# The opening of a fused attention and feed-forward kernel in another order: loads, weight preparation and transposes

## The chip, the core and the metric

The kernel runs on one core of one Trainium2 chip. A core has five engines that work side by side, each through its own list of instructions: PE (TensorE, matrix products; its weight loads are listed as PEld), DVE (VectorE), ACT (ScalarE), POOL (GpSimd) and SP (SyncE, which here only issues transfers). Engines wait for each other and for transfers through semaphores. Transfers between the large memory (HBM) and the on-chip memory run on 16 DMA engines. The metric is the time of one execution on the device in microseconds (us); a kernel's time is the median of several runs.

## The reference

Two blocks follow each other. The first is attention without a softmax: for each of 8 batches and 8 heads, a 64 x 64 matrix kv is the product of k and v over the sequence, the output is q times kv, and each row of 64 is divided by its root mean square and scaled by g_norm. The second is a feed-forward block on the 4608 x 512 result.

```python
kv = np.einsum('bhsd,bhse->bhde', k, v)              # 8 x 8 x 576 x 64
out = np.einsum('bhsd,bhde->bhse', q, kv)
rms = np.sqrt(np.mean(out * out, axis=-1, keepdims=True) + 1e-06)
attn = out / rms * g_norm
x = attn.transpose(0, 2, 1, 3).reshape(B * S, H * D) # 4608 x 512
h = x @ w_in                                         # 512 x 2048
r = np.maximum(h, 0.0)
y = (r * r) @ w_out                                  # 2048 x 512
```

All arrays are float32 at the reference's boundary, and moe_w_in and moe_w_out reach the kernel as 64-bit words (I64 in the code): the random weights are divided by a double, so they are double-precision numbers, and the kernel makes float32 numbers of them itself.

## The kernel before

**Tiles.** Tokens are taken in strips of 512 (four tiles of 128; N_STRIP = 9). A strip goes up through W_in (products into PSUM banks A, B and C, then relu and square into gt tiles) and down through W_out. The products are formed in Strassen-like sums of quarters; only the first strip goes up plainly (up_first, matmul at L588), so that it needs nothing of W_in but the converted pieces. Heads are taken in pairs: p = 0 to 3 of a batch.

**The opening.** The first strip needs batch 0's four pairs. For one pair these slices exist:

- convert_on_act(p): ACT prepares piece p of W_in, an activation to w_c (L203) and one in place on raw (L206). A piece is 128 x 512 double-precision words, one transfer of 512 KB.
- transposed_query (T in the changed code): PE transposes q by a product with the identity into t_ps (L331), ACT copies it to qT (L333).
- key_value (K): PE forms kv_ps (L349), ACT copies its two diagonal blocks into kv_all (L351, L352).
- first_queries (Q): PE forms x_ps (L419), ACT squares it into sq (L384), DVE sums to ms (L386, L387). Here also the first two of four DVE steps of a piece's conversion are issued (L215, L217).
- first_normalized (N): a third step of the conversion (L221), then ACT's square root to rms (L392), DVE's reciprocal and a Newton step (L393 to L398), the scaled x_n (L430), and the last conversion step (L224), which writes w_in.
- first_features (F): PE transposes x_n into xt_ps (L440), ACT scales it into xT (L441).

The loop over p puts them into one list: convert_on_act(p), T(p), K(p), N(p-1), Q(p), F(p-1), and N(3), F(3) at the end. attend(n) issues the list up to place n. Every engine takes its own instructions in this order: the schedule is written by hand (tc.manual_schedule()), nothing is sorted later. Before the list's last two slices the kernel issues convert_on_act for pieces 4 and 5.

**Loads.** All go through SP's queue. load_next loads k, v and the two halves of q of the next pair; load_piece loads the next piece into one of 8 raw buffers. Before the opening: the rest rows of k and v, then pair p and piece p by turns, then load_more(0) up to 8 pieces. Eight semaphores serve these loads in turn, so that a load waits for the landing of the one eight places earlier. A piece's buffer is used again when its conversion is done.

**Beside the first strip.** During the 16 up_first steps, convert(5 + (3i + 2)//4) issues the conversion of further pieces two by two, first ACT's part for a pair ahead, then DVE's four steps; pieces 24 to 31 (W_out's second half) are combined by DVE (L241) and sent back to HBM (w_out). Also batch 1's T and K are issued in the last of these steps. The first product of the next stage (query, products_x with the matmul at L373) needs all of batch 1's kv_all copies.

**Buffers.** apsum has four PSUM buffers for t_ps, kv_ps, x_ps and xt_ps; wtmp has four for w_c; fpsum holds banks A (twice), B and C.

Of the kernel before, what the change touches and what calls it, by code (L numbers as in the profile page):

```python
# [19 lines left out]
def kernel(  # L20
# [36 lines left out]
    B, H, S, D = q.shape  # L57
# [3 lines left out]
    NP = H // 2  # L61
# [35 lines left out]
    def load(b, p, q_eng):  # L97
        hs = slice(2 * p, 2 * p + 2)
        if b == 0 and p >= 2:

            h_place = g_pool.tile([P, 4, C * P], FP32, name="first_qkv", tag="gt")
        for i, (n, src, eng) in enumerate((("k", k, nc.sync), ("v", v, nc.sync), ("q", q, q_eng))):
            whole = src[b, hs, 0 : C * P].rearrange("h (sp c) d -> sp h c d", c=C)
            if n == "q" and b >= Q_ON_PE:

                t = qkv_pool.tile([P, 4 * C, SQ], FP32, name=n, tag=n)
                for a in range(4):
                    h, f = divmod(a * SQ, D)
                    eng.dma_start(
                        out=t[ts(a, SQ)],  # L110
                        in_=src[b, 2 * p + h, 0 : C * P, f : f + SQ].rearrange("(i k) f -> i k f", k=4 * C),
                    )
            elif n != "q":
                if b == 0 and p >= 2:
                    t = h_place[:, i].rearrange("p (h c d) -> p h c d", h=2, c=C)
                else:
                    t = qkv_pool.tile([P, 2, C, D], FP32, name=n, tag=n)
                eng.dma_start(out=t, in_=whole)
            else:

                if b == 0 and p >= 2:
                    t = h_place[:, i].rearrange("p (c h d) -> p c h d", h=2, c=C)
                else:
                    t = qkv_pool.tile([P, C, 2, D], FP32, name=n, tag=n)
                for h in range(2):
                    eng.dma_start(out=t[:, :, h, :], in_=whole[:, h])
            main[n, b, p] = t
# [9 lines left out]
    def load_rest(b, eng):  # L137
        h = b % 2
        half = slice(REST * h, REST * (h + 1))
        for t, src in ((k_rest[half], k), (v_rest[half, h], v)):  # L140
            eng.dma_start(out=t, in_=src[b, :, C * P : S].rearrange("h s d -> s h d"))
# [20 lines left out]
    def load_next(q_eng=nc.sync):  # L162
        u = next(to_load, None)
        if u is not None:
            load(*u, q_eng)


    KH, FH, DH = NP // 2, d_ff // 2, d_model // 2
# [4 lines left out]
    w_in = wpool.tile([P, KH, NG, 7, WN // 2], FP32, name="w_in")  # L173
# [14 lines left out]
    def load_piece():  # L188
        if len(raw) < len(sources):
            t = raw_pool.tile([P, 2, WN // 2], I64, name="raw", tag="raw")  # L190
            nc.sync.dma_start(out=t, in_=sources[len(raw)])
            raw.append(t)
# [16 lines left out]
    def conversion(i, dest):  # L209

        c, r, high = words.pop(i)
        ci = c.bitcast(I32)


        yield nc.vector.tensor_scalar(out=c, in0=c, scalar1=LEAST, scalar2=MOST, op0=ALU.max, op1=ALU.min)  # L215

        yield nc.vector.tensor_scalar(  # L217
            out=ci, in0=ci, scalar1=3, scalar2=0x3FFFFFFF, op0=ALU.logical_shift_left, op1=ALU.bitwise_and
        )

        yield nc.vector.scalar_tensor_tensor(  # L221
            out=ci, in0=high, scalar=-(2**30), in1=ci, op0=ALU.bitwise_and, op1=ALU.bitwise_or
        )
        yield nc.vector.tensor_tensor(out=dest.bitcast(I32), in0=ci, in1=r, op=ALU.add)  # L224
# [71 lines left out]
    nc.scalar.sqrt(one, one)  # L296

    load_rest(0, nc.sync)
    for p in range(NP):
        load_next()  # L300
        load_piece()
    load_more(0)
# [7 lines left out]
    flat = lambda t: t.rearrange("p h d -> p (h d)")  # L310
# [70 lines left out]
    def mean_squares(ps):  # L381
        n = ps.shape[-1] // D
        sq = xn_pool.tile([P, d_model], FP32, name="sq", tag="sq", bufs=1)
        nc.scalar.activation(sq, ps, AF.Square)  # L384
        ms = small.tile([P, H], FP32, name="ms", tag="ms")
        nc.vector.reduce_sum(out=ms, in_=by_head(sq), axis=AX.X)  # L386
        nc.vector.tensor_scalar(out=ms, in0=ms, scalar1=1.0 / D, scalar2=EPS, op0=ALU.mult, op1=ALU.add)  # L387
        return ms

    def inverse_root(ms):  # L390
        r = small.tile([P, H], FP32, name="rms", tag="rms")
        nc.scalar.activation(r, ms, AF.Sqrt)  # L392
        nc.vector.reciprocal(r, r)  # L393

        t = small.tile([P, H], FP32, name="newton", tag="newton")
        nc.vector.scalar_tensor_tensor(out=t, in0=ms, scalar=-0.5, in1=r, op0=ALU.mult, op1=ALU.mult)
        nc.vector.tensor_tensor(out=t, in0=t, in1=r, op=ALU.mult)
        nc.vector.scalar_tensor_tensor(out=r, in0=t, scalar=1.5, in1=r, op0=ALU.add, op1=ALU.mult)  # L398
        return r
# [12 lines left out]

    first = {}

    def first_queries(p):

        ps = apsum.tile([P, NT, P], FP32, name="x_ps", tag="at")
        for n in range(NT):
            nc.tensor.matmul(ps[:, n, :], lhsT=qT[0, p][:, n, :], rhs=kvd[0, p], start=True, stop=True)  # L419
        steps = conversion(p, w_in[:, p % KH, 0, p // KH * 2 : p // KH * 2 + 2])  # L420
        next(steps)
        next(steps)
        first[p] = flat(ps), mean_squares(flat(ps)), steps

    def first_normalized(p):
        ps, ms, steps = first.pop(p)
        next(steps)
        x_n["first", p] = t = xn_pool.tile([P, NT, P], FP32, name="x_n", tag="x_n")
        r = inverse_root(ms)
        nc.vector.tensor_tensor(  # L430
            out=by_head(flat(t)), in0=by_head(ps), in1=r.unsqueeze(2).to_broadcast([P, H, D]), op=ALU.mult
        )
        for _ in steps:
            pass

    def first_features(p):
        t, x = x_n.pop(("first", p)), open_xt(0)
# [47 lines left out]
        minus(nc.vector, t4, x(1, 0), t2)  # L485

    slices, ready = [], {}
    for b in range(B):
        for p in range(NP):
            if b:  # L490
                slices += [(transposed_query, (b, p)), (key_value, (b, p))]
                continue

            slices += [(convert_on_act, (p,)), (transposed_query, (b, p)), (key_value, (b, p))]
            if p > 0:
                slices.append((first_normalized, (p - 1,)))
            slices.append((first_queries, (p,)))
            if p > 0:
                slices.append((first_features, (p - 1,)))
        first_n = b // 2 * PAIR + (C if b % 2 else 0)  # L500
        ns = list(range(first_n, first_n + C + b % 2))
        if b == 0:
            slices += [(first_normalized, (NP - 1,)), (first_features, (NP - 1,))]
            ready[0] = len(slices)
            continue
        for i in range(len(ns) + 1):
            if i < len(ns):
                slices.append((query, (ns[i],)))
            if 0 < i <= len(ns):
                slices.append((features if b < X_ON_PE else squares_x, (ns[i - 1],)))  # L510
            if i > 0 and ns[i - 1] % NT == NT - 1:
                ready[ns[i - 1] // NT] = len(slices)
    slice_at = [0]

    def attend(n):
        while slice_at[0] < min(n, len(slices)):
            fn, a = slices[slice_at[0]]
            fn(*a)
            slice_at[0] += 1
# [272 lines left out]
        if k == 6 and s + 1 < N_STRIP:  # L792
            sums_x(s + 1)

    attend(ready[0] - 2)
    for i in range(NP, NP + 2):
        convert_on_act(i)
    acted[0] = NP + 2
    for s in range(N_STRIP):
        attend(ready[s])  # L800
        if s == 0:
            steps = [(2, up_first, (g, fh, i)) for g in range(NG) for fh in range(2) for i in range(2)]
        else:
            steps = [(1, up, (s, g, p)) for g in range(NG) for p in ORDER]
# [85 lines left out]
```

## Time and profile before

| | |
|---|---|
| median of 9 runs | 964.82 us (963.02 to 967.02) |
| the profiled execution's own time | 963.02 us |
| its span in the profile | 961.2 us |
| PE, DVE, ACT busy | 927.8, 644.2, 229.0 us |
| first matmul | 10.11 us |
| first matmul of the first strip's up products (L588) | 37.74 us |
| first conversion step of piece 4 on DVE | 37.29 us |
| mean granted TensorE clock | 0.992 |

Times in the profile count from the start of the span. A line of the timeline gives an instruction's start, its length, its engine and source line, the tiles it writes and reads, and, in brackets, how long its engine had been idle before it and what ended that. In the waits, a line says which engine and line waited for which, in total, how often, and the longest. ACT and DVE show starts closer together than an instruction's length: neighbours overlap in their ends, so a chain of instructions is best counted from start to start.

| us | PE busy | DVE busy | ACT busy | granted clock | GB/s |
|---|---|---|---|---|---|
| 0 to 10 | 0.00 | 1.41 | 1.49 | 1.00 | 154 |
| 10 to 20 | 7.30 | 3.37 | 4.94 | 1.00 | 323 |
| 20 to 30 | 5.66 | 7.76 | 6.57 | 1.00 | 367 |
| 30 to 40 | 4.50 | 8.13 | 5.59 | 0.54 | 104 |
| 40 to 60 | 20.00 | 20.00 | 18.63 | 0.98 | 271 |
| 60 to 80 | 20.00 | 18.48 | 18.72 | 1.00 | 311 |
| 80 to 110 | 30.00 | 27.33 | 19.93 | 1.00 | 247 |

### The profile page before, as it was taken

Reading aid. Unit: us, or ns where it says so; the run is one execution under the profiler, and the core shown is the slowest. Engines: PE = TensorE matmul, PEld = TensorE weight load, DVE = VectorE, ACT = ScalarE, POOL = GpSimd, SP = SyncE. Lnnn points to the kernel's source line nnn. Section 1 sums busy time; section 2 is a strip of 40 time slices with the busy share of each in tenths; the row PEclk is TensorE's granted clock in tenths of the full one; section 3 lists DMA queues with packets and bytes.
Section 4 is the critical chain, followed back from the end, with each engine's and each line's share of the span. In section 5 each row is a group of like instructions: output and inputs, shape, how many; then the busy total and the mean of one; then the engine's idle time right before and its main releaser. Section 6 shows DMA issues by size and latency. Waiting matters only on the chain.

```text
span 961.2 us, 15319 instructions
## 1 busy us (share of the span) xinstructions
PE 927.8 (97%) x5976; PEld 816.4 (85%) x5976; DVE 644.2 (67%) x1161; ACT 229.0 (24%) x501; POOL 1.7 (0%) x7
## 2 busy tenths in 40 slices
PE   3699999999999999999999999999999999999996
PEld 3344888888888998899889998999889988998996
DVE  3899864585437875587648874787568655863583
ACT  3697441320023002210222012201220022002200
POOL 0000000000000000000000000000000000000000
PEclk9799999999999999999999999999999999999998
DMA  8699883536975485557563765467506721671064
GB/s 256 214 294 306 271 219 146 131 113 217 313 241 122 176 299 168 123 187 251 189 152 135 248 222 153 117 240 263 134 23 239 254 88 55 230 263 55 16 227 153
DMA packets 164520, 180.33 MB, mean 188 GB/s; under 512 B 85088, under 2 KB 138848, under 8 KB 155872
## 3 DMA queue, kind: packets, MB, share of 16 engines
q1 hardware_dynamic: 164288, 179.36, 59.2%
q8 instruction: 47, 0.77, 0.3%
q14 instruction: 25, 0.20, 0.1%
q10 hardware_dynamic: 160, 0.00, 0.0%
HBM read 148.11 MB, written 31.20 MB: 187 GB/s over the span
## 4 chain that ended last, share of the span: by engine, by line
PE 95%; ACT 2%; DVE 2%; DMA 1%; issue 0%; SPq 0%; DVEq 0%
PE ps_A L552 29%; PE ps_B L552 14%; PE ps_B L736 14%; PE ps_A L736 14%; PE ps_C L552 12%; PE ps_A L588 3%; PE x_ps L378 3%; PE kv_ps L349 2%; PE ps_B L588 1%; PE ps_C L588 1%; DMA raw<-in_moe_w_in_dram 1%; PE x_ps L373 0%; PE xt_ps L440 0%; ACT w_c L203 0%; ACT raw L206 0%
## 5 line engine op out<-in xcount | busy, mean ns | idle before, releaser
L552 PE MATMUL ps_A<-x_t,w_in 128*128 128x256 f32 x768 | 182.6, 381 | 1.3 <-DVE gt L611 1.3
L552 PEld LDWEIGHTS ps_A<-x_t,w_in 128*128 128x128 f32 x768 | 143.6, 190 | 21.1 <-DVE gt L611 2.1
L736 PE MATMUL ps_B<-w_blk,g_s 128*128 128x128 f32 x672 | 81.9, 275 | 0.0
L736 PE MATMUL ps_A<-w_blk,g_s 128*128 128x128 f32 x672 | 81.9, 275 | 0.0
L736 PEld LDWEIGHTS ps_B<-w_blk,g_s 128*128 128x128 f32 x672 | 78.4, 192 | 0.0
L736 PEld LDWEIGHTS ps_A<-w_blk,g_s 128*128 128x128 f32 x672 | 78.4, 192 | 0.0
L612 DVE SCALAR_TENSOR_TENSOR gt<-gt 128x512 f32<-128x512 f32 x96 | 66.4, 692 | 3.3
L562 ACT COPY snap<-ps_A 128x512 f32<-128x512 f32 x68 | 39.8, 585 | 113.8 <-PE ps_A L552 99.3
L611 DVE TENSOR_TENSOR gt<-ps_C,snap 128x512 f32<-128x512 f32 x32 | 22.0, 688 | 64.3 <-PE ps_C L552 64.3
L736 PE MATMUL ps_B<-w_blk,gt 128*128 128x128 f32 x504 | 63.1, 275 | 0.0
L736 PE MATMUL ps_A<-w_blk,gt 128*128 128x128 f32 x504 | 63.1, 275 | 0.0
L611 DVE TENSOR_TENSOR gt<-ps_A,snap 128x512 f32<-128x512 f32 x32 | 22.0, 687 | 60.4 <-PE ps_A L552 60.3
L552 PE MATMUL ps_A<-xT,w_in 128*128 128x256 f32 x256 | 61.2, 382 | 0.0
L552 PE MATMUL ps_C<-xT,w_in 128*128 128x256 f32 x256 | 61.0, 381 | 0.0
L552 PE MATMUL ps_B<-x_t,w_in 128*128 128x256 f32 x256 | 60.9, 381 | 0.0
L241 DVE TENSOR_TENSOR gt<-gt 128x2048 f32<-128x2048 f32 (+1 forms) x31 | 58.1, 1874 | 4.0 <-PE ps_C L552 3.8
L552 PE MATMUL ps_B<-xT,w_in 128*128 128x256 f32 x256 | 60.7, 380 | 0.0
L736 PEld LDWEIGHTS ps_B<-w_blk,gt 128*128 128x128 f32 x504 | 60.2, 192 | 0.4
L736 PEld LDWEIGHTS ps_A<-w_blk,gt 128*128 128x128 f32 x504 | 60.2, 192 | 0.4
L552 PE MATMUL ps_C<-w_blk,gt 128*128 128x256 f32 x256 | 56.6, 379 | 0.0
L552 PEld LDWEIGHTS ps_C<-xT,w_in 128*128 128x128 f32 x256 | 48.1, 190 | 6.7 <-issue 0.2
L552 PEld LDWEIGHTS ps_B<-xT,w_in 128*128 128x128 f32 x256 | 48.3, 190 | 6.5
(118 smaller groups left out, 1263.2 us busy)
## 6 DMA issues: line engine op xcount, KB each, us to landing
w_blk<-w_deep SPq DMA_DIRECT2D x42, 1024.0 KB, 5.2
w_blk<-w_out SPq DMA_DIRECT2D x42, 768.0 KB, 5.0
w_blk<-w_out SPq DMA_DIRECT2D x18, 1024.0 KB, 5.2
raw<-in_moe_w_in_dram SPq DMA_DIRECT2D x16, 512.0 KB, 6.2
raw<-in_moe_w_out_dram SPq DMA_DIRECT2D x16, 512.0 KB, 5.6
k<-in_k_dram SPq DMA_DIRECT2D x30, 256.0 KB, 3.1
v<-in_v_dram SPq DMA_DIRECT2D x30, 256.0 KB, 3.7
w_deep<-w_t SPq DMA_DIRECT2D x7, 1024.0 KB, 8.8
```

Of the source, the lines that this page charges most:

```text
L241: eng.tensor_tensor(out=out, in0=a, in1=b, op=ALU.subtract)
L349: nc.tensor.matmul(ps[ts(h, D)], lhsT=a, rhs=w, start=c == 0, stop=c == C)
L378: nc.tensor.matmul(o, lhsT=qT[b, p][:, c_b, :], rhs=kvd[b, p], start=True, stop=True)
L552: nc.tensor.matmul(bank[BANK[p]][:, i, :], lhsT=lhsT(k), rhs=rhs(k), start=p in (1, 5, 2) and i == 0 and k == 0, stop=k == n - 1, skip_gro ...
L562: nc.scalar.copy(snap[p], b)
L588: nc.tensor.matmul(ps, lhsT=w_in[:, kc % KH, g, kc // KH * 2 + fh, ts(i, P)], rhs=xt[0][:, :, kc, :], start=kc == 0, stop=kc == NP - 1,)
L611: nc.vector.tensor_tensor(out=o, in0=b, in1=a, op=ALU.add)
L612: nc.vector.scalar_tensor_tensor(out=o, in0=o, scalar=0.0, in1=o, op0=ALU.max, op1=ALU.mult)
L736: nc.tensor.matmul(chain[c][x][:, i, :], lhsT=a[:, f, :], rhs=w[:, f, :], start=p not in (6, 7, 3) and j in (1, 3) and f == 0, stop=f == F ...
```

## The change

Three things are reordered; no instruction is added or left out.

1. Loads: pairs 0 and 1 are loaded ahead of piece 0, then pair 2, piece 1, pair 3, piece 2; piece 3 comes with the pieces after the pairs.
2. Pieces: convert_on_act(p) now stands behind T, K and Q of pair p, and the four DVE steps of a conversion are slices of their own (first_piece), no longer parts of Q and N.
3. Transposes: F of pair p stands one round later, behind Q of pair p + 2; the rest of the pieces' work and F(2), F(3) end the list. The whole list is issued before convert_on_act for pieces 4 and 5.

```diff
     load_rest(0, nc.sync)
-    for p in range(NP):
+    load_next()
+    for p in range(1, NP):
         load_next()
         load_piece()
     load_more(0)
@@
     def first_queries(p):
         ps = apsum.tile([P, NT, P], FP32, name="x_ps", tag="at")
         for n in range(NT):
             nc.tensor.matmul(ps[:, n, :], lhsT=qT[0, p][:, n, :], rhs=kvd[0, p], start=True, stop=True)
-        steps = conversion(p, w_in[:, p % KH, 0, p // KH * 2 : p // KH * 2 + 2])
-        next(steps)
-        next(steps)
-        first[p] = flat(ps), mean_squares(flat(ps)), steps
+        first[p] = flat(ps), mean_squares(flat(ps))
 
     def first_normalized(p):
-        ps, ms, steps = first.pop(p)
-        next(steps)
+        ps, ms = first.pop(p)
...
-        for _ in steps:
-            pass
+
+    first_steps = {}
+
+    def first_piece(i, n):
+
+        if i not in first_steps:
+            first_steps[i] = conversion(i, w_in[:, i % KH, 0, i // KH * 2 : i // KH * 2 + 2])
+        for _ in range(n):
+            next(first_steps[i])
@@
     slices, ready = [], {}
-    for b in range(B):
+
+    act, T, K, Q, N, F, piece = (
+        convert_on_act, transposed_query, key_value, first_queries, first_normalized, first_features, first_piece
+    )
+    slices += [(T, (0, 0)), (K, (0, 0)), (Q, (0,)), (act, (0,))]
+    slices += [(T, (0, 1)), (K, (0, 1)), (piece, (0, 2)), (N, (0,)), (Q, (1,)), (act, (1,)), (piece, (0, 2))]
+    slices += [(T, (0, 2)), (K, (0, 2)), (piece, (1, 2)), (N, (1,)), (Q, (2,)), (F, (0,)), (act, (2,)), (piece, (1, 2))]
+    slices += [(T, (0, 3)), (K, (0, 3)), (piece, (2, 2)), (N, (2,)), (Q, (3,)), (F, (1,)), (piece, (2, 1)), (N, (3,))]
+    slices += [(act, (3,)), (F, (2,)), (piece, (2, 1)), (piece, (3, 4)), (F, (3,))]
+    ready[0] = len(slices)
+    for b in range(1, B):
         for p in range(NP):
-            if b:
-                slices += [(transposed_query, (b, p)), (key_value, (b, p))]
-                continue
-
-            slices += [(convert_on_act, (p,)), (transposed_query, (b, p)), (key_value, (b, p))]
-            if p > 0:
-                slices.append((first_normalized, (p - 1,)))
-            slices.append((first_queries, (p,)))
-            if p > 0:
-                slices.append((first_features, (p - 1,)))
+            slices += [(transposed_query, (b, p)), (key_value, (b, p))]
         first_n = b // 2 * PAIR + (C if b % 2 else 0)
         ns = list(range(first_n, first_n + C + b % 2))
-        if b == 0:
-            slices += [(first_normalized, (NP - 1,)), (first_features, (NP - 1,))]
-            ready[0] = len(slices)
-            continue
@@
-    attend(ready[0] - 2)
+    attend(ready[0])
     for i in range(NP, NP + 2):
         convert_on_act(i)
```

## The prediction, made before the changed kernel was run

> **What bounds the kernel now.** I read the page's busy table and PE's waits after 160 us first: they say what a saved microsecond is worth.
>
> ```profile
> PE 927.8 (97%) x5976; PEld 816.4 (85%) x5976; DVE 644.2 (67%) x1161; ACT 229.0 (24%) x501; POOL 1.7 (0%) x7
> ```
>
> ```profile
> PE ps_A L552 <- DVE gt L611: 1.3, 2, 0.6
> ```
>
> The first line is busy time by engine; the second is PE's whole list of waits from 160 us on: 1.3 us in 801. PE sets the end, so what PE gains before that stays gained. The opening is the exception; I read its waits (0 to 40 us) and then its timeline.
>
> ```profile
> ACT w_c L203 <- DMA raw<-in_moe_w_in_dram: 9.0, 1, 9.0
> PE xt_ps L440 <- DVE x_n L430: 7.1, 4, 4.7
> ```
>
> (us in total, times, longest.) The timeline (start, length, instruction, idle before it and who ended it):
>
> ```profile
> 11.71 0.66 ACT L203 ACTIVATE w_c<-raw 128x512 f32<-128x512 f32 x1 [8.98 <-DMA raw<-in_moe_w_in_dram]
> 12.83 0.57 ACT L333 COPY qT<-t_ps 128x512 f32<-128x512 f32 x1
> ...
> 19.77 0.60 ACT L384 ACTIVATE sq<-x_ps 128x512 f32<-128x512 f32 x1 [1.07 <-PE x_ps L419]
> 21.14 0.69 ACT L441 ACTIVATE xT<-xt_ps,g_col 128x512 f32<-128x512 f32 x1 [0.78 <-PE xt_ps L440]
> ...
> 36.09 0.69 DVE L430 TENSOR_TENSOR x_n<-x_ps,rms 128x512 f32<-128x512 f32 x1
> 36.83 1.11 PE L440 MATMUL xt_ps<-ident,x_n 128*128 128x128 f32 x4 [4.70 <-DVE x_n L430]
> 37.74 5.20 PE L588 MATMUL ps_A<-xT,w_in 128*128 128x512 f32 x8
> ```
>
> Each round is one ring: ACT (w_c, raw, qT, kv_all, rms), DVE (rms to x_n), PE (xt_ps), ACT (xT), and again; x_ps starts 18.51, 23.80, 29.09, so 5.28 us a round. The first ring starts late because ACT stands at piece 0 until it lands (11.71) while qT's input was ready at 11.20. The real work starts at 37.74, with a slow array, as the busy time by stage shows:
>
> ```profile
> 27.60:31.00 3.40, 1.16 (x8) 0.96 0.90 330
> 31.00:34.40 3.40, 1.09 (x4) 0.50 0.39 117
> ```
>
> (The stretch, its length, PE busy, granted clock, DMA share, GB/s.) PE is mostly idle in the tail after 30 us, the clock falls to half, and the first up product pays for it. Third, the stage after, where DVE converts weights beside PE's up products:
>
> ```profile
> 37.29 0.76 DVE L215 TENSOR_SCALAR w_c<-w_c 128x512 f32<-128x512 f32 x2
> ...
> 93.98 0.68 ACT L203 ACTIVATE w_c<-raw 128x512 f32<-128x512 f32 x1 [3.71 <-DVE w_in L241]
> ...
> 102.48 0.21 ACT L352 COPY kv_all<-kv_ps 64x64 f32<-64x64 f32 x1
> ...
> 103.73 1.09 PE L373 MATMUL x_ps<-kv_all,qT_rest 128*64 128x128 f32 x16
> ```
>
> DVE is busy 58.36 of 60 us from 40 to 100. ACT works without a gap from 95.70 to that kv_all copy, and PE needs the copy at 103.73, though it shows no wait: the margin is 103.73 - 102.69 = 1.04, less 0.13 between the end of such a copy and x_ps (18.46 to 18.51 and 13.73 to 13.87 in the opening; I take the longer), so 0.9 us. This is the place that decides how much of the opening's gain is kept.
>
> **What the Trainium skill says.** "TensorE: Matmul & The Clock Gate", part 1 (the HAM clock gate): the array runs at half clock until it has been busy about one window of 3.4 us, and falls back after an idle one. The trace agrees: x_ps is 2.05 us in round 0 and 1.16 later; the first up product spans 4.99 us on the chain, the next 3.43. Same page, architectural detail: ACT and DVE take instructions strictly in order; so the 11.71 stand holds qT, as seen. "DMA: Bandwidth & Descriptors", issuing engines are not separate DMA queues: all loads share 16 DMA engines, so moving one load ahead delays another by its bytes; here the opening moves 315 to 384 GB/s, so 512 KB is some 1.6 us.
>
> **The change part by part.** No instruction and no byte is added or removed; all of it is order.
>
> *Loads.* SP now issues k, v and q of pair 1 before piece 0; piece 3 moves behind piece 2. Landings before (issue plus time to landing): piece 0 11.7, pair 1 12.4 to 14.4, piece 1 15.7, pair 2 16.4 to 18.5, piece 2 19.75, pair 3 up to 22.3, piece 3 23.8. By bytes, pair 1 comes 1.6 earlier, pieces 0, 1, 2 land near 14.1, 18.3, 22.3, piece 3 as before.
>
> *Round 0 on ACT.* qT starts at 11.3, but the two kv_all copies wait for kv_ps (ends 12.47): 12.55 and 12.77, x_ps at 13.12 instead of 13.87. Gain 0.75, not the 1.5 of qT. Then x_ps 2.05, sq 15.2 to 15.8, w_c and raw of piece 0 to 16.9 (landed 14.1), qT 16.8, kv_all to 17.7, rms, x_ps of round 1 17.76 to 18.92, sq to 19.6: still 0.75 ahead of 20.37.
>
> *The ring opened.* xT of round r now stands a round later, so ACT no longer waits for x_n. ACT's own ring: qT 0.47, copies 0.45, x_ps with its two gaps 1.5, sq 0.65, xT 0.6, w_c and raw 1.12: 4.7 to 4.8. sq of rounds 2 and 3 end at 23.4 and 28.0 (were 25.66 and 30.94). DVE's ring, start to start from the timeline: two steps of a piece 0.46 and 0.34, rms to x_n 0.90, x_n 0.61, the ms pair 0.79, and the last two steps 0.74 and 0.60 (now dependent neighbours): 4.44. From 19.65 (sq of round 1 done) DVE has work in hand always: each sq is 0.5 to 0.9 us ahead of its ms, each rms 0.7 ahead. So I sum DVE from 19.65: 2.13 (the ms pair 0.79, the end of piece 0 0.74 and 0.60) + 4.44 + 3.70 (a round less 0.74, as piece 2's third step is not followed by its fourth: 0.60 instead of 1.34) + 0.90 = 30.8 for x_n of round 3, done 31.5 (was 36.78). So xt_ps starts at 31.55 instead of 36.83: **PE is ready 5.3 us earlier**. x_n's 0.61, piece 2's last step 0.60 and the four steps of piece 3 (2.26) follow: piece 4 could start at 34.3. With a slow array xT of round 3 ends at 33.4, w_c of pieces 4 and 5 follow it now instead of standing ahead of the last rms, and w_c of piece 5 is done at 35.1 where DVE wants it at 34.6: 0.5 lost. **DVE's conversion stream is 2.5 us earlier** (34.8 against 37.29); 3.0 if the array stays fast. PE needs piece 3 about 34.8 to 36.6, it is done 34.4: no wait.
>
> *The stage after.* PE 5.3 ahead, DVE 2.5. Banks: PE needs a bank 4.7 us or more after ACT emptied it (59.85 against 55.18 the tightest), enough for a 2.8 difference; q of the last pair lands 91.7 for 95.28, margin 3.6; fast enough. The kv_all copy behind 102.48 follows ACT's two last pieces, which wait for landings (issue 88.26 plus 5.6 is 93.9, the wait that the view lays to DVE) issued behind DVE's sums on SP's queue: it moves with DVE, 2.5. So x_ps of L373 becomes a new wait of 5.3 - 2.5 - 0.9 = 1.9 us, which shows nowhere in before; behind it in PE's queue stand the second half of the first down product and all that follows. **Kept: 2.5 + 0.9 = 3.4 us.** Later margins hold: the w_blk load issued at 140.70 lands 145.5 for 149.28. On the profiled execution: 963.02 us (span 961.2 and 1.8 around it) becomes 959.6; that run is the lowest of nine, 1.8 below the median, so 964.82 becomes 961.4.
>
> *Unknown costs.* The granted clock after 30 us: if fast, PE is ready up to 7.3 earlier but only 3.9 is kept; if PE's new idle of 1.9 us drops the clock, a repeat of the start's 4.99 - 3.43 = 1.6 is lost. I take neither. Pieces landing late: below nothing is excluded, as ACT is in order; above, margin 1.2 us for pieces 0 and 1, then one for one; taken 0.
>
> **The rivals.** (a) PE keeps all of its 5.3: 959.5. For it: PE shows no wait from 40 to 134 us. Against: the 0.9 us margin. (b) Part is lost, to late pieces or to a clock that drops at the new wait (1.6): 963.0. For it: the clock fell to 0.50 at 1.16 busy of 3.4; against: it held at 1.74 (17.4 to 20.8). (c) Slower: the gate stays shut through the opening. x_ps is 2.05 instead of 1.16, xt_ps 1.1: sq of round 1 ends 21.1, ACT's ring is near 5.4 to 6, sq of round 3 at 31.7 instead of 28.0, so DVE's stream starts 0.7 later than before; 0.9 of margin leaves +0.2, and the wait at L373 drops the clock again, -1.6: 966.2. It decides when PE's busy share falls below something between 1.16 and 1.74 of 3.4; against it, my schedule has 2.5 of 3.4, denser than before. (d) The reorder changes nothing, 964.8: all but excluded, since every engine of the built program has the new order.
>
> **How the numbers follow.** Forecast 961.4: 0.54; (a) 0.14; (b) 0.21; (c) 0.08; (d) 0.03. What can be told from no change is 0.2%, 1.9 us. Faster: nearly all of the forecast's (0.50), (a) and half of (b): 0.74. Same 0.17, with (d), the rest of (b) and 0.04 of the forecast; slower 0.09. Range 959.0 to 964.6: (a) mostly and (b) inside, (c) out.
>
> **What would show it.** Right: qT ahead of w_c on ACT and x_ps near 13.1; sq of rounds 1 to 3 ending 19.6, 23.4, 28.0; DVE without idle from 20 to 34; last xt_ps at 31.5; the stream at 34.8; a PE wait near 98 to 100 us on the kv_all copy before L373's x_ps. Wrong: DVE gaps before ms (slow array or late pieces), no wait at L373 (then a), a clock of 0.5 after it (b).

## The result: 5.3 us faster, 3.4 were forecast

| | before | after |
|---|---|---|
| median | 964.83 us (963.02 to 968.03, 32 runs) | 959.56 us (958.21 to 962.32, 10 runs) |
| the profiled execution, its span | 963.02, 961.2 us | 960.3, 958.5 us |
| first x_ps of the opening starts | 13.87 us | 12.83 us |
| last xt_ps of the opening starts | 36.83 us | 31.63 us |
| first up product starts | 37.74 us | 32.12 us |
| DVE's first step of piece 4 | 37.29 us | 34.44 us |
| first product behind the x_ps of L373 (L374 after) | 104.76 us | 100.99 us |

The ratio of after to before is 0.9948, 95% interval 0.9938 to 0.9959: a gain of 4.0 to 6.0 us. Lines of the changed code stand one or two further down.

The page of the changed kernel, busy time by engine: no engine does other work than before.

```profile
PE 928.7 (97%) x5976; PEld 816.9 (85%) x5976; DVE 644.4 (67%) x1161; ACT 229.3 (24%) x501; POOL 1.7 (0%) x7
```

ACT's waits from 0 to 40 us (us in total, times, longest). The 9.0 us wait for piece 0 is gone; ACT now waits for the first t_ps.

```profile
ACT qT L334 <- PE t_ps L332: 8.2, 1, 8.2
ACT sq L385 <- PE x_ps L421: 5.7, 4, 2.2
ACT xT L446 <- PE xt_ps L445: 1.1, 2, 0.9
```

The timeline of the opening: qT runs 4.65 us ahead of w_c, where it stood behind it; the up products follow the last xt_ps.

```profile
10.93 0.59 ACT L334 COPY qT<-t_ps 128x512 f32<-128x512 f32 x1 [8.20 <-PE t_ps L332]
...
12.83 2.04 PE L421 MATMUL x_ps<-kv_all,qT 128*128 128x128 f32 x8 [0.68 <-ACT kv_all L353]
...
15.58 0.69 ACT L203 ACTIVATE w_c<-raw 128x512 f32<-128x512 f32 x1
...
31.63 0.65 PE L445 MATMUL xt_ps<-ident,x_n 128*128 128x128 f32 x4 [2.41 <-DVE x_n L428]
...
32.12 5.30 PE L590 MATMUL ps_A<-xT,w_in 128*128 128x512 f32 x8
...
34.44 0.76 DVE L215 TENSOR_SCALAR w_c<-w_c 128x512 f32<-128x512 f32 x2
```

Busy time by stage (stretch, length, PE, PEld, DVE, ACT, POOL busy, granted clock, DMA share, GB/s): from 27.6 to 34.4 DVE is busy 6.18 of 6.8 us. PE was busy 1.09 us from 31.00 to 34.40 before; it is 2.77 now, since the up products have begun.

```profile
27.60:31.00 3.40, 1.34 (x11) 0.86 (x9) 2.99 (x10) 2.67 (x6) 0.00 (x0) 1.00 1.01 372
31.00:34.40 3.40, 2.77 (x8) 1.55 (x9) 3.19 (x6) 2.46 (x5) 0.00 (x0) 0.76 0.30 110
```

And the wait that the profile of before did not show, in the timeline: PE has done 14 of the 16 products of the L374 group and stands 1.33 us at the last two, until ACT's last kv_all copy is done. PE began its up products 5.62 us earlier than before (37.74 less 32.12) and leaves this place 3.77 us earlier.

```profile
100.37 0.21 ACT L353 COPY kv_all<-kv_ps 64x64 f32<-64x64 f32 x1
...
100.63 0.43 PE L374 MATMUL x_ps<-kv_all,qT_rest 128*64 128x128 f32 x2 [1.33 <-ACT kv_all L353]
```

PE's waits from 160 us on have one entry more than before; it takes another 0.8 us of the 3.77 in this execution. At the next group of x_ps products made from qT_rest (290.62 us before, 287.91 after) 2.7 us are left of it.

```profile
PE ps_A L554 <- DVE gt L613: 1.3, 2, 0.6
PE ps_A L554 <- DVE o_sb L694: 0.8, 1, 0.8
```

### The profile page after: what moved, and what is told of

The parts are those of the page before. It is cut to its first block, busy times and chain, and to the rows that moved or that the text cites. A ratio compares the mean times of both kernels' runs of the same rounds, so it can differ in the third digit from the quotient of the medians.

```text
span 958.5 us, 15323 instructions
## 1 busy us (share of the span) xinstructions
PE 928.7 (97%) x5976; PEld 816.9 (85%) x5976; DVE 644.4 (67%) x1161; ACT 229.3 (24%) x501; POOL 1.7 (0%) x7
## 4 chain that ended last, share of the span: by engine, by line
PE 91%; DVE 3%; DMA 3%; ACT 2%; SPq 1%; issue 0%; DVEq 0%; ACTq 0%
PE ps_A L554 29%; PE ps_B L554 14%; PE ps_B L738 14%; PE ps_A L738 14%; PE ps_C L554 12%; PE x_ps L379 3%; PE kv_ps L350 2%; PE ps_A L590 1%; DMA raw<-in_moe_w_out_dram 1%; DMA raw<-in_moe_w_in_dram 1%; PE ps_B L590 1%; SPq L118 1%; DMA k_rest<-in_k_dram 1%; SPq L126 1%; DVE w_c L221 0%
## 5 line engine op out<-in xcount | busy, mean ns | idle before, releaser
L554 PEld LDWEIGHTS ps_A<-x_t,w_in 128*128 128x128 f32 x768 | 143.5, 190 | 21.3 <-DVE gt L613 2.3
L387 DVE TENSOR_REDUCE ms<-sq 128x8 f32<-128x512 f32 x36 | 24.6, 685 | 43.7 <-ACT sq L385 42.9
```

The costliest lines, as they stand in the source:

```text
L554: nc.tensor.matmul(bank[BANK[p]][:, i, :], lhsT=lhsT(k), rhs=rhs(k), start=p in (1, 5, 2) and i == 0 and k == 0, stop=k == n - 1, skip_gro ...
```

## The experiments

Theory A is the prediction's: DVE's conversion stream sets the place of L374 (the x_ps product, L373 before), so the gain is the stream's 2.5 us and PE's old margin of 0.9. Its first rival (B in the expectations) is that PE keeps the whole 5.3 us; another theory (C) came up with the result: what the forecast lacks lies in how executions of one kernel differ, by landings at the start and by transfers further on, which a single profile of before can't show. Four marks divide each profile: the first product (T of pair 0), the first x_ps, DVE's first step of piece 4, and the first product behind the x_ps of L373. A fifth is the next group of x_ps from kv_all and qT_rest, near 290 us; from there to the end all profiles take 670.60 to 670.63 us, so every difference arises ahead of it. Gains in us below are the distance of the ratio from 1 times 964.

### Does ACT's look-ahead set the wait at L374?

In the last conversions ACT takes the next pair's part ahead of the last kv_all copies and stands at its landing. The edit leaves this look-ahead out for the last pair, in the changed kernel (look_after) and in the kernel before (look_before):

```diff
-        for i in range(acted[0], min(ids[-1] + 3, len(sources))):
+        for i in range(acted[0], ids[-1] + 3 if ids[-1] + 3 < len(sources) else ids[-1] + 1):
```

> The changed kernel, but ACT's part of pieces 30 and 31 is issued with their own DVE steps and not a pair ahead, so that on ACT it stands behind the evacuation of step 13 and the kv_all copies of pair 2. Theory A (the kept gain is capped where x_ps of L374 waits for the last kv_all copy, 1.33 us in the trace of after): the copy comes about 1.9 us earlier, the wait goes, and what is late next is x_n for the transpose behind it, as DVE is busy with its sums to 101.7; some 0.9 us faster than after (about 958.7). Theory B (PE keeps its whole head start anyway and that wait is slack elsewhere): no change, 959.6.

> The same edit in the kernel before. Theory A: PE reaches that x_ps 0.9 us after the copy there, so the edit frees nothing: 964.8, within 0.3. Theory B, or a general merit of the edit: faster by the same amount as in the changed kernel.

look_after: 959.20 us, ratio 0.9947 (0.9932 to 0.9962), not to be told from the changed kernel; A had expected 958.7. Its waits of PE from 100 to 300 us:

```profile
PE kv_ps L350 <- DMA v<-in_v_dram: 0.7, 1, 0.7
PE xt_ps L458 <- DVE x_n L406: 0.7, 1, 0.7
...
PE x_ps L374 <- ACT kv_all L353: 0.4, 1, 0.4
```

The wait fell from 1.3 to 0.4 us, as A says: the last kv_all copy starts 5.03 us behind ACT's start on the last piece, where it was 6.79. But other waits are in the profile now, for a normalized x_n and for a load of v. look_before: 964.16 us, ratio 0.9997 (0.9989 to 1.0006). There the copy has its margin, so nothing follows, as A expects. The wait at L374 is real, but no gain from shortening it was measured; with intervals of 1.4 us to each side the 0.9 that A expected is not excluded.

### Does DVE's stream or PE's start set the gain?

Both add work that nothing uses, between the opening and the pieces: two memsets on DVE (dve_plus), or one 128x512 product on PE ahead of the up products (pe_plus).

```diff
+    spare = xn_pool.tile([P, d_model], FP32, name="spare", tag="sq", bufs=1)
+    for _ in range(2):
+        nc.vector.memset(spare, 0.0)
```

```diff
+    ps = apsum.tile([P, NT, P], FP32, name="spare", tag="at")
+    nc.tensor.matmul(ps.rearrange("p n t -> p (n t)"), lhsT=ident, rhs=k_rest.rearrange("p h d -> p (h d)"), start=True, stop=True)
```

> The changed kernel with two memsets of a spare 128x512 tile on DVE between the opening and the conversion of piece 4, some 0.9 us of DVE work that nothing reads. Theory A (DVE's conversion stream sets when the last kv_all copy comes): the wait at L374 grows by 0.9 and the kernel is 0.9 slower than after, 960.5. Theory B (PE's own start sets it): no change, 959.6.

> The changed kernel with one more 128x512 product on PE (two passes, 0.86 us at full clock, up to 1.7 at half) between the last transpose of the opening and the first up product; nothing reads it. Theory A: the wait at L374 shrinks by as much (1.33 us to about 0.4 or to nothing) and the kernel's time stays, 959.6, within 0.4. Theory B: slower by 0.9 to 1.7, 960.5 to 961.3.

dve_plus: 960.76 us, ratio 0.9962 (0.9948 to 0.9975), 1.3 us less gain than the changed kernel, with intervals that overlap. In the timeline the two memsets put 1.2 us between the first steps of piece 3 and piece 4 (33.09 to 36.64, which is 3.55 against 2.35):

```profile
35.58 0.48 DVE L800 MEMSET spare<- 128x512 f32 x1
...
36.24 0.48 DVE L800 MEMSET spare<- 128x512 f32 x1 [0.17 <-DVE spare L800]
...
36.64 0.69 DVE L215 TENSOR_SCALAR w_c<-w_c 128x512 f32<-128x512 f32 x2
```

The product behind L374's x_ps comes at 102.70. In the first profile of the changed kernel it came at 100.99, but in a second one without any edit (after_2, below) at 102.60, so this place alone does not show DVE's part. The chain that leads to it does (start times in us):

| | pieces 6 and 7 on DVE, first step | the last two raw loads issued | ACT starts on the second piece | last kv_all copy | product behind x_ps |
|---|---|---|---|---|---|
| before | 41.04 | 88.26 | 95.70 | 102.48 | 104.76 |
| after | 38.19 | 85.91 | 93.58 | 100.37 | 100.99 |
| after_2 | 39.34 | 87.01 | 95.19 | 101.97 | 102.60 |
| dve_plus | 40.33 | 88.07 | 95.28 | 102.08 | 102.70 |
| pe_plus | 39.46 | 87.20 | 93.70 | 100.48 | 101.10 |
| look_after | 39.26 | 86.92 | 95.14 | 100.17 | 100.79 |

The issue follows DVE's stream by 47.66 to 47.74 us in all five profiles of the changed opening, and the copy follows ACT's start on the last piece by 6.78 to 6.80 us in all but look_after, whose edit lies there. Between them stand two transfers, and from their issue to ACT's start on the second piece it is 6.50 to 8.22 us. That scatter is as large as what was added on DVE: dve_plus issued 1.06 us later than after_2, but its transfers were 0.97 us shorter. ACT's stand at the first of the two, in after_2 and then in dve_plus:

```profile
93.90 0.68 ACT L203 ACTIVATE w_c<-raw 128x512 f32<-128x512 f32 x1 [4.93 <-DMA raw<-in_moe_w_out_dram]
```

```profile
93.23 0.68 ACT L203 ACTIVATE w_c<-raw 128x512 f32<-128x512 f32 x1 [3.12 <-DMA raw<-in_moe_w_out_dram]
```

So DVE sets the issue one for one, as A says, and a landing that the forecast took as fixed (5.6 us) decides as much about the place.

pe_plus: the up products start at 35.07, 2.95 us later than in the first profile of the changed kernel and 1.80 later than in after_2 (33.27), yet at L374 nothing of it is left: the product behind it comes at 101.10 us (100.99 and 102.60), again right behind ACT's copy, and the timeline shows all 16 products in one go, with no wait listed (1.32 us; the same 16 took 1.09 in before):

```profile
99.85 1.32 PE L374 MATMUL x_ps<-kv_all,qT_rest 128*64 128x128 f32 x16
...
100.48 0.21 ACT L353 COPY kv_all<-kv_ps 64x64 f32<-64x64 f32 x1
```

That speaks against the rival that PE keeps its head start: 1.8 us of it or more can be thrown away without moving this place. But the whole time was a miss for A: 961.87 us, ratio 0.9969 (0.9957 to 0.9981), about 2 us slower where 0 was expected. In its profile they are lost between 200 and 300 us:

```profile
PE ps_A L554 <- DMA w_blk<-w_out: 1.3, 1, 1.3
PE ps_B L554 <- DVE o_sb L694: 0.9, 1, 0.9
PE kv_ps L350 <- DMA v<-in_v_dram: 0.3, 1, 0.3
```

Waits of this kind come and go from kernel to kernel (below); whether the extra product brings them about was not settled.

### How much do two executions of one kernel differ?

No edit: the kernel before twice more, and the changed kernel once more.

> The kernel before, profiled again. The first profile of before was the fastest of its runs (963.02 against a median of 964.83) and showed no PE wait on transfers between 230 and 290 us; runs of the changed kernel and its variants showed 0.8 to 2.5 us of such waits there. Theory C (the stretch from 230 to 290 us, where weight blocks are loaded just in time, adds 0 to 2.5 us from run to run in every kernel, and the median gain of 5.3 is the 3.8 gained by 105 us plus luck of the draw): this profile shows such waits of 1 to 2.5 us, or a slower opening. Theory D (the changed kernel gains in that stretch too): no such waits here either, and the time is like the first profile's.

> The kernel before once more, for the same question: theory C expects between its place at 105 us and the first profile's a difference under 1 us, and waits on transfers from 230 to 290 us that differ from those of the other two profiles; theory D expects none.

> The changed kernel, profiled and timed again. Theory A: the wait of x_ps of L374 on the last kv_all copy is there again (1 to 2 us) and PE stands 3.4 to 4 us earlier than in the first profile of before behind it. Theory C: the PE waits on transfers from 230 to 290 us differ from those of the first profile (0.95 us) by up to 1.5 us. Time 959.6 within 1.

after_2: 959.96 us, ratio 0.9949 (0.9935 to 0.9962). In its profile the wait at L374 is 0.97 us, but the place lies 2.2 us ahead of the first profile of before (104.76 less 102.60), where A expected 3.4 to 4; PE waits for no transfer from 230 to 290 us. The two of before took 963.48 and 966.51 us in the profile. before_2 has no such waits either, which is D's case, but its first x_ps is 0.7 us later, which is C's. before_3 passes L373 1.2 us later than the first profile, a little more than C allowed, and waits 1.2 us for a w_blk. Where ACT stands at piece 0 (before_3), the timeline reads:

```profile
13.27 0.66 ACT L203 ACTIVATE w_c<-raw 128x512 f32<-128x512 f32 x1 [10.54 <-DMA raw<-in_moe_w_in_dram]
...
15.43 1.83 PE L419 MATMUL x_ps<-kv_all,qT 128*128 128x128 f32 x7 [3.01 <-ACT kv_all L352]
```

Piece 0 held ACT until 13.27 us here, until 11.71 in the profile on which the prediction rests. All stretches, in us (the mean of the four that share before's opening, with look_before; and of the three that share the changed one, with after_2 and look_after; the edit of the look pair lies in the fourth stretch):

| stretch | forecast gain | first pair of profiles | before, mean | after, mean | gain of the means |
|---|---|---|---|---|---|
| to the first product | 0 | 0.31 | 10.19 | 9.87 | 0.32 |
| to the first x_ps | 0.75 | 0.73 | 4.42 | 3.03 | 1.39 |
| to piece 4 on DVE | 1.75 | 1.81 | 23.33 | 22.01 | 1.32 |
| to the product behind L373's x_ps | 0.9 | 0.92 | 67.56 | 66.56 | 1.00 |
| to the next such group, near 290 | 0 | -1.06 | 186.32 | 186.74 | -0.42 |

Without the look pair the fourth row is 0.39 and the fifth 0.27, from three and two profiles. In the second row the two openings differ most clearly: in the four profiles of before's opening the first x_ps came 3.76, 4.71, 5.36 and 3.87 us behind the first product; with the changed opening always 3.02 or 3.03. In before it is the landing of a 512 KB transfer; after, a chain of engine work. For the start this supports C: the profile that the sum was made against had the earliest first x_ps of four (13.87, against 14.56, 14.59 and 15.43 us).

### Which part of the change brings what?

f_undone puts F of pair p behind Q of pair p + 1, as before; loads_undone loads piece 0 ahead of pair 1 again; pieces_only does both, so that of the change only the places of convert_on_act and of the DVE steps are left; loads_only gives the kernel before the new loads and nothing else. Their edits (of the first, one of four lines in which F moves):

```diff
-... (N, (0,)), (Q, (1,)), (act, (1,)), (piece, (0, 2))]
+... (N, (0,)), (Q, (1,)), (F, (0,)), (act, (1,)), (piece, (0, 2))]
```

```diff
-    load_next()
-    for p in range(1, NP):
+    for p in range(NP):
```

> The changed kernel with the transposes in their old round: F of pair p behind Q of pair p + 1, everything else as changed. Theory A: ACT's xT waits for x_n of the same round again, so the ring closes; rounds 2 and 3 take 5 us or more instead of 4.4, the conversion of piece 4 starts about 1 to 1.5 us later, and the kernel is as much slower than after (about 960.8). Rival (the start alone, pieces behind the copies, brings the gain): no change, 959.6.

> The kernel before with the new order of loads alone: pair 1 is loaded ahead of piece 0, all else as before. Piece 0 lands about 1.6 us later (pair 1's 512 KB at 315 to 384 GB/s), and ACT still stands at it ahead of the first qT. Theory A (what the opening gains comes from ACT no longer standing at the piece and from the opened ring): the first x_ps of L419 starts 1 to 2 us later than in the kernel before (15.5 to 16.5 us, against 13.9 to 15.4 in four profiles of it), DVE's first step of piece 4 moves by the same to about 39.5, and the time is 1 to 2 us above before's: about 966. Rival: the loads' order brings a gain of its own, since pairs 1 to 3 come earlier; the time is below before's, 962 to 963.

> The changed kernel with the loads in their old order (piece 0 ahead of pair 1, piece 3 behind pair 3). Theory A: ACT takes pair 0 ahead of piece 0 by its own order, so the first x_ps of L420 stays at 12.6 to 13.2 us; pair 1 lands up to 14.4 while its copy is wanted near 16.8; so DVE's first step of piece 4 stays at 34.4 to 35.2 and the time at 959.6, within 0.5 of the changed kernel. Rival: the start needs the pair ahead of the piece; sq of round 1 comes about 1.5 us later, piece 4 at 36 or later, the time 961 or above.

> Of the three parts of the change only the pieces' places: loads as before, transposes F of pair p behind Q of pair p+1 as before. Theory A: as the run with F alone undone, since the loads matter little: first x_ps near 13, DVE's first step of piece 4 near 36.6, time 962.2, within 0.7 of that run, so 2 to 3 us below before's. Rival (the three parts need each other, no gain from one alone): 964.4, as before.

| | median | ratio, interval | gain | first product | to first x_ps | to piece 4 |
|---|---|---|---|---|---|---|
| loads_only | 966.44 us | 1.0034 (1.0019 to 1.0048) | -3.3 | 9.82 | 6.58 | 23.45 |
| pieces_only | 962.38 us | 0.9984 (0.9971 to 0.9998) | 1.5 | 10.49 | 3.03 | 23.60 |
| f_undone (loads and pieces) | 962.24 us | 0.9980 (0.9967 to 0.9993) | 1.9 | 10.19 | 3.03 | 23.35 |
| loads_undone (pieces and F) | 960.31 us | 0.9970 (0.9957 to 0.9983) | 2.9 | 11.45 | 3.03 | 21.28 |
| all three | 959.56 us | 0.9948 (0.9938 to 0.9959) | 5.0 | 9.80 | 3.03 | 21.61 |

The columns at the right, in us, are of one profile each. The stand at piece 0 goes with the pieces' places alone (6.58 or 3.8 to 5.4, against 3.03). The round of 5.28 us goes with F alone: without it, 23.4 to 23.6 from the first x_ps to piece 4, as in before (23.0 to 23.5); with it, 21.3 to 22.6 (dve_plus aside, which adds to this stretch). f_undone shows the old round in its timeline, x_ps 23.14 and 28.42, 5.28 apart:

```profile
23.14 1.16 PE L421 MATMUL x_ps<-kv_all,qT 128*128 128x128 f32 x8 [1.53 <-ACT kv_all L353]
...
28.42 1.16 PE L421 MATMUL x_ps<-kv_all,qT 128*128 128x128 f32 x8 [1.53 <-ACT kv_all L353]
```

By the timings the F part is clear of the noise with the new loads: f_undone gains 0.7 to 3.2 us, all three parts 4.0 to 6.0. But f_undone was expected at 960.8 and took 962.24, and its profile, the fastest of its runs (960.42 us), does not show where that time goes: its span is 958.6 us, that of the changed kernel 958.5. pieces_only came out within 0.7 us of f_undone, as expected, but 1.5 us below before instead of 2 to 3.

The loads alone do harm, as expected, and more than the 1 to 2 us that were named: ACT stands at a piece that lands later still, 14.24 us in loads_only. (The expectation counts 512 KB for a pair; k, v and q of a pair are 768 KB.)

```profile
14.24 0.66 ACT L203 ACTIVATE w_c<-raw 128x512 f32<-128x512 f32 x1 [11.51 <-DMA raw<-in_moe_w_in_dram]
14.81 0.66 ACT L206 ACTIVATE raw<-raw 128x512 int32<-128x512 uint32 x1
15.37 0.56 ACT L334 COPY qT<-t_ps 128x512 f32<-128x512 f32 x1
```

loads_undone was expected within 0.5 us of the changed kernel; it is 0.7 above by the medians, 2 by the ratios. Its rival named the wrong place: sq of round 1 starts 3.9 us behind that of round 0 (4.0 in the changed kernel), so pair 1 is in time. What is late is the very first product, at 11.45 us, and with it the first x_ps (14.48, where 12.6 to 13.2 was expected) and piece 4 on DVE (35.76, expected 34.4 to 35.2). With the loads in the old order it starts at 9.88 to 11.45, mean 10.45 in six profiles; with the new, at 9.61 to 10.19, mean 9.83 in seven. The transfers right behind pair 0's are other ones and q of pair 0 lands some 0.6 us earlier. The ranges overlap, so this is likely rather than shown; it is also the only difference that these profiles show for the loads. By the timings F brings 1.4 us with the old loads and 3.1 with the new, the loads 0.4 without F and 2.1 with it; with intervals of 1 us and more to each side, whether the two help each other stays open.

### A version that starts earlier still

With ACT no longer at the piece, the 3.03 us from the first product to x_ps are T, then K and its two copies. k and v of pair 0 land ahead of q, so K can go first:

```diff
-    slices += [(T, (0, 0)), (K, (0, 0)), (Q, (0,)), (act, (0,))]
+    slices += [(K, (0, 0)), (T, (0, 0)), (Q, (0,)), (act, (0,))]
```

> The changed kernel with K of pair 0 ahead of T of pair 0, on PE and on ACT. In twelve of the profiles so far that take pair 0 ahead of piece 0, or could, the first product waits for q, and in those with the changed opening the first x_ps starts 3.0 us behind it, since kv_ps and its two copies stand behind T and qT. k and v of pair 0 land about 8.0 to 8.5 us, q about 9.8; so kv_ps can be done when q lands, and x_ps follows T and qT alone: 1.09 for t_ps and 0.6 for qT. Theory A (the start moves the conversion stream on DVE one for one, and the place of L374 stands 66 us behind that): first product near 8.2, first x_ps near 11.6 instead of 12.8 to 13.0, piece 4 on DVE 33.2 to 34.2, the first product behind L374's x_ps 1.2 earlier, near 100.5; time 958.4, if the later transfers keep up. Rival: piece 0 (landing 14.2) and pair 2 are late next, or the start's gain is given back at L374 or at the transfers near 250 us; 959.6 as the changed kernel, or above.

958.55 us, ratio 0.9942 (0.9928 to 0.9955). The opening does what was expected:

```profile
8.02 1.12 PE L350 MATMUL kv_ps<-v,k 128*64 128x64 f32 x16 [8.02 <-DMA v<-in_v_dram]
...
9.56 1.08 PE L332 MATMUL t_ps<-ident,q 128*128 128x128 f32 x4 [0.20 <-DMA q<-in_q_dram]
11.41 2.05 PE L421 MATMUL x_ps<-kv_all,qT 128*128 128x128 f32 x8 [0.77 <-ACT qT L334]
```

x_ps is 1.4 us earlier, piece 4 is at 33.10 (34.44), the product behind L374's x_ps at 100.11 (100.99). But in the profile it is given back, as the rival had it, at two transfers before 252 us:

```profile
PE ps_A L554 <- DMA w_blk<-w_out: 1.5, 1, 1.5
PE ps_B L554 <- DMA w_blk<-w_out: 0.7, 1, 0.7
```

Its median is 1.0 us under the changed kernel's and the lowest measured; the intervals overlap, so a further gain is not shown.

A pattern stands behind this, seen but not tested. Of the nine profiles with the changed pieces, four pass L374 by 101.1 us (k_first, look_after, the changed kernel, pe_plus); all four then wait between 200 and 300 us, and take 186.9 to 188.8 us to the group near 290. Five pass it at 102.6 to 102.9; four of them take 185.5 us, without such a wait, and one (loads_undone) 187.9. So k_first, the changed kernel, dve_plus and f_undone reach the group near 290 at 288.6, 287.9, 288.2 and 288.0, though they passed L374 at 100.1, 101.0, 102.7 and 102.6. The pair after_2 and look_after says the same: with piece 4 at 35.18 and 35.09 us they pass L374 at 102.60 and 100.79, and reach the group near 290 at 288.1 and 288.6, so 1.8 us at L374 were worth nothing there. It looks like a second place that decides, the transfers of 230 to 260 us, where the DMA engines are busy 84 to 99% in the changed kernel.

## Why the prediction was right, and where it fell short

**The start.** Forecast x_ps 13.1, measured 12.83; the step of 0.75 from the first product measured 0.73 in the pair of profiles it was worked out for. This is the step that was mis-sized: it took one landing of piece 0, in the profile of the execution that was the lowest of nine, for the kernel's. Over four profiles the stand costs 0.64 us more, 1.39.

**The loads.** Costed at nothing as long as pieces landed in time. They did in the first profile (dve_plus and pe_plus show stands of 0.54 and 0.34 us at piece 0); that the order also touches q of pair 0, which is ahead of all that was moved, was not thought of: likely, though not shown, 0.3 us in the mean of the profiles, 0.6 in the wider comparison.

**The opened ring.** sq of rounds 1 to 3 ended 19.5, 23.8 and 28.6 us (forecast 19.6, 23.4, 28.0), x_n of round 3 started 30.88 (30.8), the last xt_ps 31.63 (31.55), DVE's piece 4 34.44 (34.8). ACT's ring was some 0.3 longer than summed in this profile, and DVE hid it. So the opened ring came out as the sum has it, in the execution that was profiled first. The trace also agrees with the in-order rule for ACT and DVE that the prediction took from the Trainium skill, "TensorE: Matmul & The Clock Gate", architectural detail: moving the w_c of piece 0 behind the copies freed exactly what stood behind it.

**The clock.** The first up product, eight instructions, took 5.30 us (5.20 before): the array was as slow at this point as before, as taken. Over the nine profiles with the changed pieces it took 3.99 to 6.11. But the forecast also took the array as fast in rounds 1 to 3, and there luck came in. In the first profile x_ps of round 1 took 1.16 us; in after_2, look_after, dve_plus and pe_plus it took 2.08, as long as in round 0. sq of round 1 then ends later (20.43 us in after_2, 19.53 in the first profile), and DVE stands at its ms, which the prediction had named as a sign of being wrong:

```profile
17.66 2.08 PE L421 MATMUL x_ps<-kv_all,qT 128*128 128x128 f32 x8 [0.53 <-ACT kv_all L353]
...
20.46 0.69 DVE L387 TENSOR_REDUCE ms<-sq 128x8 f32<-128x512 f32 x1 [0.98 <-ACT sq L385]
```

Piece 4 stood at 34.44 us in the first profile and at 35.09 to 35.27 in the three of these four that add nothing on DVE. The profile's clock column reads 1.00 in that stretch, as it does in round 0, so what slowed the product is not shown. In the first profile the array slowed a round later: the granted clock was 0.75 from 20.8 to 27.6 us, x_ps of round 2 took 1.40 us, and DVE still had work.

The prediction lets the array fall back after an idle window. In the traces the window ahead was not idle: the granted clock fell at 30.7 us in before, after PE had been busy 1.42 of 3.41 us (27.30 to 30.71), and at 22.5 us in the changed kernel, after 1.68 of 3.41 us.

**The cap at L373.** Forecast a new wait of 1.9 us there; measured 1.33 and 0.97 in two profiles. The margin of 0.9 came out as 0.92 in the pair. That PE arrives 5.6 us earlier and leaves 3.8 earlier is shown for this pair; with after_2 it is 2.2. What holds PE there is the copy, as forecast (pe_plus, look_after); but the prediction moved the copy with DVE alone, and the landings ahead of it add 6.5 to 8.2 us, not a fixed time. Rival (a) named a time of 959.5, which is what came out, but for a reason that does not hold: PE does not keep its 5.3 us.

**After L373.** The prediction held that this place decides what is kept and that later margins hold, for a w_blk load among others. That failed in these profiles: from L374 to the group near 290 the changed kernel lost 1.06 us in the pair, and of the nine profiles with the changed pieces, which pass L374 between 100.1 and 102.9 us, seven came out within 0.7 us of each other there (287.9 to 288.6).

**The sum.** At the place of L373 it reads 0 + 0.75 + 1.75 + 0.9 = 3.4 in the forecast, 3.77 in the pair, and 0.32 + 1.39 + 1.32 + 1.00 = 4.0 in the means (3.65 without the look pair). Near 290 it is 2.7 in the pair and 3.6 in the means (3.9 without the look pair). The rest of the way to the timed 5.3 is not assigned: the three profiled executions with the changed opening lay 0.5 to 1.8 us above the medians of their kernels. The low end of the measured interval is 4.0. So the forecast of 3.4 fits what the profiles hold better than the timed gain, and that the time came out 2 us lower stays unexplained.

## What to carry to other kernels

When an engine with a strict order stands at a transfer, its cost is a distribution: look at several profiles before it goes into a sum. Here the change replaced a landing (3.8 to 5.4 us) by a chain of engine work (3.0), and so gains the mean, not the case at hand. A head start on the busiest engine is not kept by itself: follow it to the first place where the engine meets a slower stream, and then to the next one, since here a second place, near 250 us, took back 1.1 of the 3.8 us that the first had let through (and in k_first all that it had gained at the first). And an order of loads may be worthless or harmful (3.3 us slower here) until the consumer's order is changed with it.

## What the runs showed that was not expected

Transfers issued behind a load seem to delay it: q of pair 0 is issued at the same time in all kernels (4.57 or 4.58 us), and lands 0.6 us later in the mean when a 512 KB piece follows rather than k, v and q of the next pair; the ranges overlap. And three executions of the same kernel before differ by up to 3.5 us (963.02, 963.48, 966.51): in the longest, 1.6 more from the first product to the first x_ps than in the shortest, and 1.2 for one w_blk transfer near 250 us.
